# First product of the last feed-forward layer over pairs of token chunks: 512-column matmuls in place of 256-column ones

## The chip, the cores and the metric

The kernel runs on one core of a Trainium2 chip. The metric is the device time of one execution in microseconds (us), lower is better. A core has five engines with instruction queues of their own: TensorE (PE, matrix products; its weight loads are shown as PEld), VectorE (DVE), ScalarE (ACT), GpSimd (POOL) and SyncE (SP, which here issues the transfers). They work side by side and wait for one another through semaphores. Matmuls write to PSUM, eight banks of 128 partitions x 512 fp32 columns.

## The reference

```python
x = A_x                                          # 1 x 2048 x 512
x = x + _A_ref(_layernorm(x), A_wqkv, A_wo)      # linear attention, 32 heads
x = x + _B_ref(_layernorm(x), B_w1, B_w2)        # relu(x @ w1) @ w2, hidden width 1376
x = x + _A_ref(_layernorm(x), A_wqkv, A_wo)
x = x + _B_ref(_layernorm(x), B_w1, B_w2)
```

Linear attention takes `phi(t) = t+1 for t>0, else exp(t)` of queries and keys, multiplies the queries by the sum of key-value products of each head, divides by the normaliser and projects with `wo`. The four layers are numbered 0 to 3; layers 1 and 3 are the feed-forward ones, with the same weights.

## The kernel before

**Tiles and chunks.** The 2048 tokens are 16 tiles of 128, and four chunks of 512 tokens. The residual `xres` stays in SBUF in fp32. Each layer normalises a tile to `xn` (fp16). Pairs of tiles are transposed by DMA from `xn` to `Tb`, so that the feature dimension lies on the partitions: a chunk is complete after two such transposes.

**The end of an attention layer** (function `layer_steps`, steps `bar` and `p2`). The key-value sums are masked to one head each (`kvmask`, L1159) and multiplied into the output weights (`m0` to `m3`), whose four results are evacuated to `Mf`. The projection of tile i (`fin`, four matmuls of 512 columns with weights from `big` and moving data from `Mf`) is added to the residual on VectorE (`resid`, L960). ScalarE squares the row (`sq`, L968). GpSimd and VectorE turn sums into mean, variance, `rstd` and `nbias` for two tiles at once (`ln_stats`); then each tile is normalised (`norm`, L890 on VectorE or GpSimd, L895 on ScalarE), and SP issues the transpose (`tr`, L900). For the four tiles of chunk 0 the projection is split in two halves: the first halves (`fin0_0` to `fin3_0`) and the second ones (`fin0_2` to `fin3_2`), which need `m2` and `m3`. In the tail of `bar` there is also the normaliser of the last chunk (`den3`, four matmuls over 32-column blocks, which the profile shows as `big,Zc`).

**The first product of a feed-forward layer** (`b_h7`). The hidden width of 1376 is split into 2 x 5 feature chunks of 128 (`KH` = 5) and a rest of 96 columns. The rest is computed on its own (`b_h_rest`: `hr`, 16 matmuls of 96 columns a chunk, clipped at zero and transposed by DMA, `trh`). The ten feature chunks are computed by the Winograd form of Strassen's product, with seven block products in place of eight. The blocks of the input are two halves of a chunk's tokens (256 each) by two halves of the 512 features: a11, a12 for the first tokens, a21, a22 for the last. The blocks of the weights are the two halves of the features by the two halves of the hidden width. VectorE makes four sums of the input blocks (`hs1` to `hs4`, L1402, written to `xn`):

    s1 = a21 + a22    s2 = s1 - a11    s3 = a11 - a21    s4 = a12 - s2

Four sums of the weight blocks, t1 to t4, are made once. For each group of feature chunks, `[0,1]`, `[2,3]` and `[4]`, three banks are used. Bank BA takes product 1 (a11), is copied by ScalarE to bank BB (`hv1`, L700), then takes products 6 (s2), 7 (s3) and 4 (a22) on top. BB takes product 2 (a12) on top of the copy. BC takes product 5 (s1), is saved to SBUF (`hv5`, L1455), then takes product 3 (s4). BA is also saved after product 6 (`hv6`). The four results are clipped or added, on ScalarE or VectorE (`hc11`, `hc12`, `hc22`, `hc21`; L1424, L1425, L1436; the clip of two added quarters, `hc22r`, is L1445 or L1446). With two feature chunks a group, a bank holds two blocks of 256 columns, and a product is four matmuls of 256 columns; for the group `[4]` it is two. Products 1 and 2 read the first tokens only; 3 to 7 need the last tokens or the sums.

**The second product** (`b_out`) is a seven-term product too, per chunk, with sums over the hidden values made on VectorE (`b_out_sums`: `ssum1` to `ssum5`, L1509) and terms `p1` to `p7`. `p1` reads the first half of the hidden features for the first tokens, `p5` the sum `ssum1`, `p2` the second half of the features. Its results are added to the residual (L1602), and in the last layer written to staging tiles (L1616, L1610) and stored. `ssum` values are written into the chunk's `Tb` and `xn`.

**The order.** A planner (`_list_schedule`) lays the instructions out for each engine by a priority: the position at which the program text adds the operation, plus a hand-tuned number from the table `HINTS`. `WINDOW` is 1 for every engine, so each engine takes its operations strictly by that sum; entries with `!` choose the engine of an operation that can run on several. Banks are given out as they come free, and semaphore waits follow from reads and writes. The steps of two layers are interleaved: `layer_steps` gives each step the chunk that it needs and the chunk that it provides. Around the start of layer 3 the program text runs: `p2` of chunk 0, first product of chunk 0, `p2` of chunk 1, first product of 1, `p2` of 2, second product of 0, `p2` of 3, first product of 2, second of 1, first of 3, second of 2, second of 3.

Of the kernel before, what the change touches and what calls it, by code (L numbers as in the profile page):

```python
# [7 lines left out]
ALU = alu_op_type.AluOpType  # L8
# [8 lines left out]
C_MM512 = 216.0  # L17
# [45 lines left out]
HINTS = {"0.aqsum1": -43, "0.aqsum1!": 0, "0.aqsum2": -24, "0.aqsum2!": 0, "0.aqsum3": -126, "0.aqsum3!": 0, "0.aqsum4": 36,  # L63
# [545 lines left out]
def build_kernel(nc, A_x, A_wqkv, A_wo, B_w1, B_w2, out, n_layers_pairs=2, K_STT=0, Q_STT=0, windows=None,  # L609
# [20 lines left out]
    with es:  # L630
# [64 lines left out]
        def alloc_bank(cols=512, need=0):  # L695
            return g.new_tile(cols, need)
# [54 lines left out]
        def h_unit(c, t):  # L751
            return c * NCH + t
# [1222 lines left out]
```

## Time and profile before

| | us |
|---|---|
| median of 3 runs (lowest to highest) | 263.33 (263.28 to 263.78) |
| profiled execution, whole time | 262.21 |
| profiled execution, span from first to last instruction | 260.5 |
| TensorE busy / weight loads | 255.3 / 198.9 |
| VectorE busy | 230.7 |
| ScalarE busy | 207.5 |
| GpSimd busy | 60.0 |
| TensorE's granted clock, mean | 1.000 |

Time is counted from the first instruction of the profiled execution. A matmul's own duration in the profile (273 ns for 256 columns, 380 for 512) includes the way through the array, which the next matmul overlaps; what a stream costs is read from the starts of its members. A row such as `177.16 13.11 PE L953 MATMUL ps<-Mf,big 128*128 128x512 bf16 x60` of the engines' order of time gives the start, the length of the stretch, the line, the output tile with its inputs, the shape and how many instructions are merged. All grouped matmuls carry L953, the line of the helper, so their inputs tell them apart: `Tb,w`, `xn,w`, `xn,xin` and `Tb,xin` are the products of layer 3's first product (input blocks or sums by weights or weight sums), `w,Tb` with 96 columns the rest, `w,big` and `xin,big` and the like with bf16 the second product. A SyncE issue is `SPq`; where a DMA's landing matters, the views of a tile give the time from issue to landing.

### The profile page before, as it was taken

The numbers are of one execution on the slowest core, as the hardware profiler recorded it, in microseconds if no ns is written. First come the engines' busy times: TensorE is split into PE (matmuls) and PEld (weight loads), VectorE is DVE, ScalarE is ACT, GpSimd is POOL, SyncE is SP. The second block draws the span as 40 slices with busy tenths as digits, with TensorE's granted clock in tenths as the row PEclk, the third lists the DMA queues.
The fourth block names the chain that finished last, engine by engine and source line by source line (L and its number), as shares of the span: only waits on it lengthen the run. The fifth ranks groups of instructions, "written<-read, shape, count | busy, mean of one in ns | idle before, by whom it ended". The sixth has DMA issues, their size and how long they took to land.

```text
span 260.5 us, 5888 instructions
## 1 busy us (share of the span) xinstructions
PE 255.3 (98%) x2176; PEld 198.9 (76%) x2176; DVE 230.7 (89%) x574; ACT 207.5 (80%) x446; POOL 60.0 (23%) x160
## 2 busy tenths in 40 slices
PE   7999999999999999999999999999999999999995
PEld 3555577834778898889888878774488988988884
DVE  4999998799989999999999899759999997876874
ACT  4999999579989988998899799786999946882200
POOL 4110000028745007240330340002875000000000
PEclk9999999999999999999999999999999999999999
DMA  7767951744351430434031030057442514200104
GB/s 206 277 148 140 330 189 21 183 101 97 68 67 32 87 58 12 91 42 63 0 60 25 0 73 11 3 113 172 95 80 50 82 23 128 56 20 3 81 3 161
DMA packets 45980, 22.46 MB, mean 86 GB/s; under 512 B 35872, under 2 KB 44416, under 8 KB 45952
## 3 DMA queue, kind: packets, MB, share of 16 engines
q1 hardware_dynamic: 45680, 21.83, 35.8%
q8 instruction: 17, 0.28, 0.4%
q10 hardware_dynamic: 272, 0.26, 0.4%
q14 instruction: 11, 0.09, 0.1%
HBM read 7.14 MB, written 2.10 MB: 35 GB/s over the span
## 4 chain that ended last, share of the span: by engine, by line
PE 85%; ACT 5%; DVE 4%; DMA 4%; SPq 1%; issue 1%
PE ps L953 84%; DVE xres L960 2%; DMA Tb<-xn 2%; SPq L1227 1%; ACT sqscr L968 1%; DMA big<-rdc 1%; DMA xin<-in_A_x_dram 1%; ACT xn L895 1%; DVE bst L847 1%; PE ps L914 0%; ACT rdc L1217 0%; DVE big L1235 0%; ACT escr L935 0%; ACT ps L700 0%; ACT lnd L1215 0%
## 5 line engine op out<-in xcount | busy, mean ns | idle before, releaser
L953 PE MATMUL ps<-w,big 128*128 128x256 bf16 (+1 forms) x256 | 32.3, 273 | 0.0
L968 ACT ACTIVATE sqscr<-xres 128x512 bf16<-128x512 f32 x48 | 29.8, 622 | 3.2 <-DVE xres L1623 1.6
L953 PE MATMUL ps<-big,xn 128*128 128x256 bf16 (+1 forms) x224 | 32.1, 288 | 0.0
L700 ACT ACTIVATE ps<-ps 128x512 f32<-128x512 f32 (+1 forms) x41 | 23.1, 573 | 10.5 <-PE ps L953 10.2
L953 PE MATMUL ps<-Mf,big 128*128 128x512 bf16 x128 | 28.6, 380 | 0.0
L953 PEld LDWEIGHTS ps<-w,big 128*128 128x128 bf16 (+1 forms) x256 | 25.0, 98 | 3.1
L953 PEld LDWEIGHTS ps<-big,xn 128*128 128x128 f16 x224 | 21.4, 98 | 6.3 <-issue 1.1
L953 PE MATMUL ps<-Tb,w 128*128 128x256 f16 x160 | 24.3, 273 | 0.0
L1436 DVE TENSOR_TENSOR big<-ps,escr 128x512 bf16<-128x512 f32 (+1 forms) x38 | 22.7, 601 | 1.3 <-ACT escr L1455 0.6
L953 PEld LDWEIGHTS ps<-Mf,big 128*128 128x128 bf16 x128 | 12.2, 98 | 14.5 <-ACT Mf L1166 0.5
L953 PE MATMUL ps<-xn,w 128*128 128x256 f16 x160 | 23.0, 273 | 0.0
L953 PE MATMUL ps<-xn,xin 128*128 128x256 f16 x160 | 22.7, 273 | 0.0
L953 PE MATMUL ps<-wqkv,Tb 128*128 128x512 bf16 (+1 forms) x96 | 20.3, 344 | 0.2 <-ACT Tb L920 0.2
L895 ACT ACTIVATE xn<-xres,nbias,rstd 128x512 f16<-128x512 f32 x24 | 19.1, 813 | 1.4 <-POOL nbias L879 1.4
L1455 ACT ACTIVATE escr<-ps 128x512 f32<-128x512 f32 (+1 forms) x38 | 18.7, 535 | 1.8 <-PE ps L953 1.8
L877 POOL TENSOR_TENSOR rstd<-veps,nhalf 128x2 f32<-128x2 f32 x24 | 18.2, 759 | 7.0 <-DVE veps L875 5.5
L869 POOL TENSOR_SCALAR mean<-s 128x2 f32<-128x2 f32 x24 | 7.2, 301 | 54.4 <-DVE xres L960 52.8
L1424 ACT ACTIVATE big<-ps 128x512 bf16<-128x512 f32 (+1 forms) x38 | 18.9, 527 | 0.4 <-PE ps L953 0.3
L953 PE MATMUL ps<-w,Tb 128*128 128x96 bf16 (+2 forms) x176 | 17.3, 225 | 0.6 <-DMA Tb<-xn 0.6
L953 PEld LDWEIGHTS ps<-Tb,w 128*128 128x128 bf16 x160 | 15.5, 98 | 2.3 <-DVE w L1384 0.2
L1445 ACT ACTIVATE big<-big 128x1024 bf16<-128x1024 bf16 (+1 forms) x16 | 14.3, 904 | 3.5 <-DVE big L1436 3.3
L953 PEld LDWEIGHTS ps<-xn,w 128*128 128x128 bf16 x160 | 15.5, 98 | 1.9 <-DVE xn L1402 0.2
(146 smaller groups left out, 639.6 us busy)
## 6 DMA issues: line engine op xcount, KB each, us to landing
big<-rdc SPq DMA_DIRECT2D x32, 128.0 KB, 2.7
xin<-in_A_x_dram SPq DMA_DIRECT2D x3, 512.0 KB, 7.0
w<-in_B_w_dram SPq DMA_DIRECT2D x1, 1376.0 KB, 7.0
w<-in_B_w_dram SPq DMA_DIRECT2D x1, 1280.0 KB, 10.1
wqkv<-in_A_wqkv_dram SPq DMA_DIRECT2D x3, 256.0 KB, 4.6
wqkv<-in_A_wqkv_dram SPq DMA_DIRECT2D x1, 512.0 KB, 4.5
wo<-in_A_wo_dram SPq DMA_DIRECT2D x1, 512.0 KB, 4.2
out_dram<-GT SPq DMA_DIRECT2D x1, 512.0 KB, 2.6
```

Source lines behind the costliest of these rows:

```text
L700: g.add(ACT, lambda e: e.activation(psv[:, b, 0:w], psv[:, src, 0:w], ACTF.Identity), [("ps", src)], [("ps", b)], C_ACT_PSUM if w == 512 e ...
L847: g.add(DVE, lambda e: e.bn_stats(bst[:, i, :], xin[:, i, :]), [("xin", i)] + list(after), [("bst", i)], C_DVE_BNST, name="bnst%d" % i)
L869: g.add(POOL, lambda e: e.tensor_scalar(mean[:, sl], s1[:, sl], -INV_D, None, ALU.mult), [("s1", i) for i in tl], [("mean", i) for i in tl ...
L877: g.add(POOL, lambda e: e.tensor_tensor(rstd[:, sl], veps[:, sl], nhalf[:, 0:n], ALU.pow), [("veps", lo), ("nhalf",)], [("rstd", i) for i ...
L895: (ACT, lambda e: e.activation(xn[:, i, :], src, ACTF.Identity, scale=rstd[:, i:i + 1], bias=nbias[:, i:i + 1]), C_ACT_SB_AP)],
L953: last = e.matmul(o, l, r, start=st, stop=sp, skip_group_check=skip)
L960: g.add(DVE, lambda e: e.scalar_tensor_tensor(xres[:, i, :], psv[:, b, :], 0.0, src, ALU.add, ALU.add, accum_out=s1[:, i:i + 1]), [("ps", ...
L968: g.add(ACT, lambda e: e.activation(sqscr[:, q, :], xres[:, i, :], ACTF.Square, scale=math.sqrt(INV_D), accum_out=s2[:, i:i + 1]), xr(i), ...
L1424: g.add_flex([(ACT, lambda e: e.activation(ap, src(), ACTF.Relu), C_ACT_PSUM if w == 512 else 270.0), (DVE, lambda e: e.tensor_scalar(ap, ...
L1436: g.add(DVE, lambda e: e.tensor_tensor(ap, sh(psv[:, bank, 0:w]), sh(other()), ALU.add), [("ps", bank)] + okeys + ([] if first else bk), q ...
L1445: g.add_flex([(ACT, lambda e: e.activation(row, row, ACTF.Relu), 945.0 if len(cs) == 2 else C_ACT_SB), (DVE, lambda e: e.tensor_scalar(row ...
L1455: g.add(ACT, lambda e, w=w: e.activation(q[:, 0:w], psv[:, bank, 0:w], ACTF.Identity), [("ps", bank)], key, C_ACT_PSUM if len(cs) == 2 els ...
```

## The change

In layer 3 the first product is computed over pairs of chunks (0 with 1, 2 with 3). The first tokens of the seven-term product are then a whole chunk of 512 tokens, the last tokens the next chunk. Each of the five feature chunks is a group by itself, a bank holds one block of 512 columns, and a product is two matmuls of 512 columns. `b_h7_pair` is `b_h7` with these blocks; the operand sums are 1024 elements a partition. The rest columns of both chunks are added at the head of the pair. Layer 1 keeps the old form (`H_PAIR`).

The steps of layer 3 change with it: the pair (0, 1) needs both chunks and comes after `p2` of chunk 1; the text now runs `p2` of 0, `p2` of 1, first product of 0 and 1, `p2` of 2, second product of 0, `p2` of 3, second of 1, first of 2 and 3, second of 2, second of 3.

The planner gets GpSimd as a third choice for the normalisation of a tile, in all layers. The table of hints is replaced: entries of the old first product go, entries of the new one come, and many of the others have new numbers (181 of layer 0's, 37 of layer 1's, 272 of layer 2's, 100 of layer 3's, and 24 choices of an engine). By position plus hint, TensorE's order at the seam is now:

- before: `den3`, `fin1_0`, `fin2_0`, `m2`, `m3`, `fin0_0`, `fin3_0`, second halves, `fin` of tiles 5, 4, 6, 7, 9, 8, 10, 11, 15, 12, 13, 14, then product 1 of groups [0,1] and [2,3], `hr0`, product 5 of [4], product 2, product 5 twice, product 6 twice of chunk 0
- now: `den3`, `m2`, `m3`, `fin0_0`, `fin1_0`, `fin0_2`, `fin1_2`, `fin3_0`, `fin2_0`, `fin3_2`, `fin2_2`, `fin` of tiles 4 to 8, 11, 9, 13, 12, 10, 14, 15, then product 1 of feature chunks 0 and 1, `hr0`, product 2 of 0 and 1, `hr1`, product 5 of 0 and 1, and so on; at the pair's end product 7 of feature chunk 4, product 4 of 3, `hr2`, `p1` of chunk 0, product 4 of 4, `p5` of chunk 0

VectorE's new order there is: `kvmask1`, a scaling of the queries, `mev2`, another scaling, `resid` 0, 1, a scaling, 3, 2, a scaling, 4, 5, 6, `veps2`, a scaling, 7, `var4`, a scaling, `nbias2`, `veps4`, 8, 9, `var6`, `nbias4`, `veps6`, `norm4`, 11, `nbias6`, 10, 12. ScalarE's is: `sq` 0, 1, 3, 2, 4, `norm1`, `sq5`, `norm0`, `sq7`, `norm2`, `sq6`, `sq9`, `norm5`, `sq8`, `norm6`. `norm3` and `norm7` are on GpSimd, as before.

```diff
-                        (ACT, lambda e: e.activation(xn[:, i, :], src, ACTF.Identity, scale=rstd[:, i:i + 1], bias=nbias[:, i:i + 1]), C_ACT_SB_AP)],
+                        (ACT, lambda e: e.activation(xn[:, i, :], src, ACTF.Identity, scale=rstd[:, i:i + 1], bias=nbias[:, i:i + 1]), C_ACT_SB_AP), ts],
...
+        H_PAIR = {1: False, 3: True}
...
+        def b_h7_pair(q, tw):
+            t1, t2, t3, t4 = tw
+            u0, u1 = 2 * q, 2 * q + 1
+            b_h_rest(u0, 1)
+            b_h_rest(u1, 1)
...
+            lo, hi = slice(4 * u0, 4 * u0 + 4), slice(4 * u1, 4 * u1 + 4)
+            a11, a12, a21, a22 = Tb[:, lo, 0:2, :], Tb[:, lo, 2:4, :], Tb[:, hi, 0:2, :], Tb[:, hi, 2:4, :]
+            kl, kh = [("T", 4 * u0 + i) for i in range(4)], [("T", 4 * u1 + i) for i in range(4)]
...
+                g.add(DVE, lambda e, o=o, a=a, b=b, op=op: e.tensor_tensor(o, a, b, op), rd, wr, C_DVE_TT2, name="%s_p%d" % (nm, q))
+
+            def prod(name, bank, W, X, c, opens, reads):
+                def mk():
+                    return [(psv[:, bank, :], W[:, d, 128 * c:128 * c + 128], X[:, :, d, :], opens and d == 0, d == 1, True) for d in range(2)]
...
+            for c in range(KH):
+                BA, BC = alloc_bank(), alloc_bank()
+                nm = "_p%d_%d" % (q, c)
+                prod("h1", BA, b11, a11, c, True, kl)
+                BB = seed(BA, 512, "hv1" + nm)
+                prod("h5", BC, t1, s1_, c, True, ks[0] + [("uw", 1)])
+                v5 = save("hv5", BC, c)
+                prod("h2", BB, b21, a12, c, False, kl)
+                relu(c, u0, BB, "hc11" + nm)
+                prod("h6", BA, t2, s2_, c, False, ks[1] + [("uw", 2)])
+                v6 = save("hv6", BA, c)
+                prod("h3", BC, b22, s4_, c, False, ks[3])
+                prod("h7", BA, t3, s3_, c, False, ks[2] + [("uw", 3)])
+                add(c + KH, u0, BC, v6, "hc12" + nm)
+                add(c + KH, u1, BA, v5, "hc22" + nm)
...
+                prod("h4", BA, t4, a22, c, False, kh + [("uw", 4)])
+                relu(c, u1, BA, "hc21" + nm)
...
+                if H_PAIR[layer]:
+                    for q in range(NCH // 2):
+                        steps.append((2 * q + 1, None, lambda q=q: h_pair(q)))
+                        for t in (2 * q, 2 * q + 1):
+                            steps.append((NCH - 1 if first_b and t == 0 else None, None if last_layer else t, lambda t=t: o_step(t)))
+                    return steps
```

More of the change, by code (lines that the diff above doesn't have):

```diff
@@ L1835, in h_step, with h_pair @@
                     sums[t] = b_out_sums(t)
+                def h_pair(q):
+                    if not tw7:
+                        tw7.append(w1_sums())
+                    b_h7_pair(q, tw7[0])
+                    for t in (2 * q, 2 * q + 1):
+                        sums[t] = b_out_sums(t)
+                if H_PAIR[layer]:
+                    for q in range(NCH // 2):
+                        steps.append((2 * q + 1, None, lambda q=q: h_pair(q)))
+                        for t in (2 * q, 2 * q + 1):
+                            steps.append((NCH - 1 if first_b and t == 0 else None, None if last_layer else t, lambda t=t: o_step(t)))
+                    return steps
                 for t in range(NCH):
```

29 lines of the change are left out of this document (28 added, 1 removed), and 502 rows, old and new, of the table HINTS.

## The prediction, made before the change was run

> **What bounds the kernel now.** I read the page first, then the chain of waits in order of time, then TensorE's waits, then its order of time around the last feed-forward layer.
>
> ```profile
> PE 255.3 (98%) x2176; PEld 198.9 (76%) x2176; DVE 230.7 (89%) x574; ACT 207.5 (80%) x446; POOL 60.0 (23%) x160
> ...
> 70.18 4.40 DMA Tb<-xn
> 74.58 0.14 issue
> 74.71 183.07 PE ps L953 x1674
> 257.79 0.02 issue
> 257.81 0.43 DVE rdc L1610
> ...
> PE ps L953 <- DMA Tb<-xn: 0.6, 1, 0.6
> ```
>
> The first row is the page's, the next five are the chain of waits (start, length), the last is TensorE's only wait from 74 us on. From 74.71 us to the end 1674 matmuls stand behind one another, 183 us without a gap. So a us of TensorE work saved there is a us of time, and any wait that the change puts in front of a matmul is paid in full. Nothing can be gained there by shortening other engines' work; the hole that ends at 74.71 is the only one left after the start-up and the first attention layer.
>
> TensorE in order of time (start, stretch, count) shows the pace and the place where the last layer begins.
>
> ```profile
> 174.77 0.38 PE L953 MATMUL ps<-wo,KVT 128*128 128x512 bf16 x1
> 175.08 0.40 PE L953 MATMUL ps<-big,Zc 128*32 128x512 bf16 x4
> 175.41 0.62 PE L953 MATMUL ps<-GT,wqkv 128*128 128x128 bf16 x8
> 175.87 1.03 PE L953 MATMUL ps<-Mf,big 128*128 128x512 bf16 x4
> 176.73 0.60 PE L953 MATMUL ps<-wo,KVT 128*128 128x512 bf16 x2
> 177.16 13.11 PE L953 MATMUL ps<-Mf,big 128*128 128x512 bf16 x60
> 190.11 1.04 PE L953 MATMUL ps<-Tb,w 128*128 128x256 f16 x8
> 190.99 0.84 PE L953 MATMUL ps<-w,Tb 128*128 128x96 bf16 x16
> 191.67 0.38 PE L953 MATMUL ps<-xn,xin 128*128 128x256 f16 x2
> ...
> 226.94 2.13 PE L953 MATMUL ps<-xn,xin 128*128 128x256 f16 x18
> 228.90 0.60 PE L953 MATMUL ps<-Tb,w 128*128 128x256 f16 x4
> ```
>
> **Pace: -0.28 us.** The starts of successive rows give the pace. Sixty 512-column matmuls take 190.11 - 177.16 = 12.95 us, 215.8 ns each; eighteen 256-column ones 228.90 - 226.94 = 1.96 us, 108.9 ns. The change takes out 4 chunks x 5 feature chunks x 7 products x 2 = 280 matmuls of 256 columns and puts in 2 x 5 x 7 x 2 = 140 of 512. Each pair becomes 2 x 108.9 - 215.8 = 2.0 ns cheaper: 0.28 us. Rows are rounded to 0.01 us, so 0 to 0.45. That is all that the change can give by itself.
>
> The Trainium skill ("TensorE: Matmul & The Clock Gate", section "Back-to-back issue gap") also gives a sustained figure of about 131 ns for N=512 in a stream with weight loads; by it the 140 matmuls would cost some 12 us less than at 215.8 ns. The 60 matmuls above are such a stream, each with its own weight load, and show 215.8, so I give that result no chance.
>
> **Work off the path: 0.** For each kind of evacuation (VectorE's additions, by form and mean ns, stand for all) the change has ten full 512-column groups instead of eight full and four half ones.
>
> ```profile
> L1436 DVE TENSOR_TENSOR big<-ps,escr 128x512 bf16<-128x512 f32 x12 | 8.1, 685 | 0.3 <-PE ps L953 0.2
> ...
> L1436 DVE TENSOR_TENSOR big<-ps,escr 128x256 bf16<-128x256 f32 x6 | 2.5, 416 | 0.0
> ```
>
> Two full ones for four halves is 1.37 for 1.66 us. The operand sums become eight VectorE additions of 1024 elements (0.69, row at 176.58 below) instead of sixteen of 512 (0.43, row at 196.99 below). So both engines get a little less to do; it is covered by TensorE's full queue either way, with VectorE at 89% and ScalarE at 80%. The hints also move some normalisations to GpSimd (tiles 8 and 12 of the second attention layer, tile 13 of the first feed-forward); their transposes are wanted far later, and GpSimd stands at 23%. Uncovered, each would cost 0.77 to 1.30 us (below).
>
> **The start of the last layer: +0.55 us.** Before, the first product runs on one chunk's transposes. Now, products 3 to 7 of a pair need chunk 1 as well; only products 1 and 2 read chunk 0 alone. The order on TensorE follows from the diff (position in the program plus hint, with no look-ahead): after the last projection matmul of the attention layer come product 1 for two feature chunks, the rest-columns of chunk 0, product 2 twice, then the rest-columns of chunk 1, then product 5. So the work in front of the first need of chunk 1 is 4 x 0.432 + 0.68 (191.67 - 190.99) = 2.41 us, from 190.11 to 192.52.
>
> ```profile
> L900 SPq DMA_TRANSPOSE Tb<-xn x2: 1249/1259/1269, 185.8 to 187.2; - x2
> DMA to landing us min/median/max: 3.1/3.1/3.2
> ...
> L900 SPq DMA_TRANSPOSE Tb<-xn x2: 1232/1260/1289, 192.3 to 193.7; - x2
> DMA to landing us min/median/max: 3.2/3.2/3.3
> ...
> 178.66 0.69 DVE L960 SCALAR_TENSOR_TENSOR xres<-ps,xres 128x512 f32<-128x512 f32 x1
> ...
> 179.28 0.69 DVE L960 SCALAR_TENSOR_TENSOR xres<-ps,xres 128x512 f32<-128x512 f32 x1
> ...
> 184.28 1.50 ACT L895 ACTIVATE xn<-xres,nbias,rstd 128x512 f16<-128x512 f32 x2
> ...
> 187.01 0.61 ACT L968 ACTIVATE sqscr<-xres 128x512 bf16<-128x512 f32 x1
> ...
> 185.67 1.30 POOL L890 TENSOR_SCALAR xn<-xres,mean,rstd 128x512 f16<-128x512 f32 x1
> ...
> 189.86 0.77 POOL L890 TENSOR_SCALAR xn<-xres,mean,rstd 128x512 f16<-128x512 f32 x1
> ...
> 196.99 0.43 DVE L1402 TENSOR_TENSOR xn<-Tb 128x512 f16<-128x512 f16 x1
> ```
>
> Now chunk 1's second transpose is issued at 193.7 and lands at 196.9. Left so, TensorE would wait 4.4 us. The new hints pull it forward. The two matmuls that fold the value mask into the output weights (176.73) come ahead of all projection halves, and tile 0's second half is third among these. The 64 projection matmuls end at 190.11, so they begin 13.81 us earlier at 176.30, tile 0 is complete at 177.6, and its residual addition can start at 177.8 instead of 178.66. VectorE's operations of 0.69 follow each other at 0.62 (178.66, 179.28). In its new order ten stand before the residual of tile 7, which ends at 177.8 + 6.2 + 0.69 = 184.7; that of tile 4 is seventh and ends at 182.2. ScalarE is the slower queue from there: after the square of tile 4 (182.85) come the norm of 1, the square of 5 and the norm of 0 (0.70, 0.62, 0.70), until 184.9; then the squares of tiles 7, 6, 9 and 8 (4 x 0.61), the norms of 2 and 5 (2 x 0.70) and that of 6 (0.80): 189.55. The transpose is issued at 189.65 and lands at 192.85, 0.33 us after TensorE runs dry. Chunk 1's rest-columns (0.68) then run while VectorE makes the first sum of 1024 elements (0.69, and an estimated 0.2 for the hand-overs, as between 175.87 and 176.07), so product 5 waits 0.2 more: 0.55 in all. Ends: 0 if only tile 7's own chain counted (190.5 landed), 1.4 if VectorE does not get its 0.86 us lead. SP's queue holds nothing new ahead of these transposes. What queues behind the wait is all of TensorE's list.
>
> **The step before it: +0.27 us.** Before, the mask of the key-value product is covered by two projection halves (the four matmuls at 175.87). The new order puts only the four normaliser matmuls there.
>
> ```profile
> 176.07 0.42 DVE L1159 TENSOR_TENSOR KVT<-ps,bmask 128x256 bf16<-128x256 f32 x1
> ...
> 176.58 0.69 DVE L1235 TENSOR_TENSOR big<-big 128x1024 bf16<-128x1024 bf16 x1
> ```
>
> The last key-value matmul issues until 175.87, the mask ends at 176.49, the next matmul could start at 176.56: 0.69 us, of which the normaliser matmuls cover 175.41 - 174.99 = 0.42 (mode changes included). 0.27 remain. Ends: 0 to 0.4. The halves still have to run, only behind, so nothing of it comes back.
>
> **The end of the first pair: +0.1 us.** Chunk 0's hidden values are complete only when the pair is, and the second product's fifth term needs the sum over them.
>
> ```profile
> L1509 DVE TENSOR_TENSOR Tb<-big 128x1280 bf16<-128x1280 bf16 x4 | 3.3, 821 | 0.5 <-ACT big L1424 0.5
> ...
> L1359 DVE TENSOR_SCALAR hr<-ps 128x384 bf16<-128x384 f32 x2 | 1.1, 550 | 0.0
> ...
> L1446 DVE TENSOR_SCALAR big<-big 128x1024 bf16<-128x1024 bf16 x2 | 0.8, 416 | 0.0
> ```
>
> VectorE after the last seventh product: 0.2 to see it, 0.62 to add, 0.42 to clip, the rest-columns' clip (ready at 1.31, ends 1.86), the sum 0.82: 2.7 us and 0.1 to hand over. TensorE has, by the new order, two fourth products (2 x 0.43), the rest-columns of chunk 2 (0.68) and the first output product (12 matmuls of 256 columns, 1.31): 2.85. Even, so 0.1, with 0 to 0.4. The second pair ends with more cover (another output product of 10 matmuls, 1.09, for the rest-columns), and the two chunks' sums that VectorE then holds at once fit into the 17 us of output products that remain.
>
> **The sum.** -0.28 + 0 + 0.55 + 0.27 + 0.1 = +0.64 us. The profiled execution is 262.21 us (span 260.5 and 1.7 around it); it becomes 262.85, its span 261.1. The median of the runs, 263.33, is 1.12 above that execution; the same step from there gives 263.97, say 264.0. Its own range, from the terms' ends without the extremes together, is 263.6 to 264.6.
>
> **Rivals.** A difference under 0.2% (0.53 us) can't be told from none.
>
> No new wait: the pulled-forward chain lands in time and the mask is covered. For it: the transposes of chunk 1 need only start 0.5 us earlier than I put them. Against: ScalarE's queue above is full. Then only the pace counts, 263.05.
>
> The hole at 74 us closes as well. It is a transpose that took 4.4 instead of 3.2 us.
>
> ```profile
> q8 instruction: 1, 0.02, 1.3%
> q14 instruction: 1, 0.01, 0.4%
> ...
> Tb<-xn SPq DMA_TRANSPOSE x1, 4.4
> ```
>
> In that window of 5 us an instruction transfer ran beside it. With 3.2 it would have landed 1.2 us earlier and hidden the 0.8 to 0.9 us between the matmuls there. The first attention and feed-forward layers keep their TensorE program and nearly all hints, so the transfer should meet the same transpose; if it doesn't, 263.33 - 0.28 - 0.85 = 262.2. The Trainium skill ("Runtime: NRT & Kernel Launch", "Instruction fetch mechanics") says that an engine's instructions are refilled in blocks of 256 over a DMA queue of its own; TensorE's 2176 matmuls and 2176 loads are exactly 17 such blocks, the page's count on q8, so the block at 72 us should stay where it is.
>
> Chunk 1 arrives late: GpSimd's norm of tile 3 or 7 takes 1.30 instead of 0.77, VectorE's lead is lost, or the transpose itself meets an instruction transfer (1.2). Each alone moves the landing by 0.5 to 1.2 us, all of it paid: 264.0 + 1.2 = 265.2. It decides from the moment the landing passes 192.9.
>
> **How the numbers follow.** My forecast 0.42 (two thirds of it beyond +0.2%), no new wait 0.25, the closed hole 0.14, late chunk 1 0.19. Faster: 0.14 and 0.04 of the second, 0.18. Same: 0.21 of the second and 0.14 of the first, 0.35. Slower: 0.28 and 0.19, 0.47. Range 262.7 to 265.2: it leaves out most of the closed hole and the worst of late landings.
>
> **What would show it.** Right: 240 matmuls of 512 columns become about 380, at 215.8 ns; a wait of 0.3 to 0.6 us in all, on the transposes before chunk 1's rest-columns and on the first sum behind them, some 2.4 us after the last projection matmul; about 0.3 us idle before the output product of the values; the rest of the last layer gapless. Wrong: the transposes land before TensorE runs dry, or TensorE has gaps inside a pair, where I expect none, since each group's chain of evacuations is as long as before.

## The result and the profile after

The changed kernel takes 264.36 us (median of 19 runs, 263.2 to 266.33), the kernel before 262.42 us (19 runs, 261.52 to 263.78) beside it on the same chip. The ratio is 1.0068, with a 95% interval of 1.0053 to 1.0084: 1.8 us slower (1.4 to 2.2). The prediction counted from 263.33 us, the median of three runs of the kernel before; in these 19 runs that kernel has 262.42. The profiled execution of the changed kernel has a span of 262.1 us against 260.5.

The page of the changed kernel, engines' busy times (eleven matmul records are missing, 2025 of 2036):

```profile
PE 254.4 (97%) x2025; PEld 184.4 (70%) x2036; DVE 230.5 (88%) x564; ACT 201.9 (77%) x431; POOL 62.2 (24%) x161
```

TensorE is still what bounds the kernel; the span is longer because TensorE waits more. The chain of waits of the changed kernel (start, length, what):

```profile
70.26 5.31 DMA Tb<-xn
75.57 0.14 issue
75.70 77.66 PE ps L947 x738
...
193.70 0.57 issue
194.28 0.69 DVE xn L1485
194.97 0.05 issue
195.01 64.51 PE ps L947 x476
```

Before, one stretch ran from 74.71 us to 257.78. Now the stretch begins at 75.70, the chain leaves TensorE for a sum on VectorE in front of 195.01, and it ends at 259.52, 1.74 us later. (Where matmul records are missing, from 153 us on, the chain also strays to other engines; those pieces mean nothing.) The first difference comes long before the layer that was changed. TensorE's waits in the changed kernel show it:

```profile
PE ps L947 <- DMA Tb<-xn: 1.5, 1, 1.5
...
PE ps L947 <- DVE KVT L1153: 0.2, 1, 0.2
```

The first row was 0.6 us before. It is the hole at 74 us, in layer 1, where the transpose of chunk 1 now takes 5.31 us in place of 4.40. In TensorE's order of time (the start, the stretch, and in brackets the idle time before it):

```profile
73.82 0.38 PE L947 MATMUL ps<-Tb,w 128*128 128x256 f16 x2
75.70 0.84 PE L947 MATMUL ps<-w,Tb 128*128 128x96 bf16 x16 [1.50 <-DMA Tb<-xn]
```

The DMA view of the changed kernel from 70 to 76 us (queue, packets, MB, share; then the transpose with its us to landing):

```profile
q14 instruction: 2, 0.02, 1.6%
q8 instruction: 1, 0.02, 1.4%
...
Tb<-xn SPq DMA_TRANSPOSE x1, 5.3
```

Before, one packet on q14 ran at 67.5 us, ahead of this transpose, and the next at 73.9. In the changed kernel the two run at 73.5 and 73.9, both inside the transpose.

TensorE in order of time in the changed kernel, at the two places that the prediction named:

```profile
176.56 0.40 PE L947 MATMUL ps<-big,Zc 128*32 128x512 bf16 x4
177.16 0.60 PE L947 MATMUL ps<-wo,KVT 128*128 128x512 bf16 x2 [0.21 <-DVE KVT L1153]
...
191.49 1.03 PE L947 MATMUL ps<-Tb,w 128*128 128x512 f16 x4
192.35 0.84 PE L947 MATMUL ps<-w,Tb 128*128 128x96 bf16 x16
193.03 1.03 PE L947 MATMUL ps<-Tb,w 128*128 128x512 f16 x4
194.05 0.85 PE L947 MATMUL ps<-w,Tb 128*128 128x96 bf16 x16
195.01 1.90 PE L947 MATMUL ps<-xn,xin 128*128 128x512 f16 x8
```

From start to start: the normaliser matmuls take 0.60 us until the next one starts, against 0.33 before (175.08 to 175.41), so the mask costs 0.27. At the entry of the last layer product 2 takes 1.02 against product 1's 0.86 (0.15 of waiting by the single records), and chunk 1's rest-columns 0.96 against chunk 0's 0.68 (0.27): 0.42 in all.

Measured from start to start between TensorE's single matmuls (the "single records" below), the 1.74 us between the two profiled executions divide so:

| where | before | after | difference |
|---|---|---|---|
| start to 74 us | | | +0.12 |
| hole at 74 us | 0.80 | 1.66 | +0.86 |
| mask in the last attention layer | 0 | 0.27 | +0.27 |
| first projection halves behind it (178.3) | 0 | 0.08 | +0.08 |
| last layer, first product to last matmul | 67.66 | 68.02 | +0.36 |

The last row holds +0.42 at the entry, +0.20 in three gaps of 0.05, 0.05 and 0.10 us (197.4, 197.9 and 258.6), and -0.28 of pace. 0.05 us are left over, within the rounding of such sums.

### The profile page after: what moved, and what is told of

Read it like the earlier page. It is cut to its first block, busy times and chain, and to the rows that moved or that the text cites. A ratio compares the mean times of both kernels' runs of the same rounds, so it can differ in the third digit from the quotient of the medians.

```text
span 262.1 us, 5551 instructions
## 1 busy us (share of the span) xinstructions
PE 254.4 (97%) x2025; PEld 184.4 (70%) x2036; DVE 230.5 (88%) x564; ACT 201.9 (77%) x431; POOL 62.2 (24%) x161
## 4 chain that ended last, share of the span: by engine, by line
PE 80%; DMA 6%; ACT 5%; DVE 4%; SPq 2%; issue 1%
PE ps L947 80%; DVE xres L954 2%; DMA big<-rdc 2%; DMA Tb<-xn 2%; DMA xin<-in_A_x_dram 2%; SPq L1221 1%; ACT sqscr L962 1%; ACT lnd L1209 1%; ACT rdc L1211 1%; ACT xn L889 1%; DVE big L1229 1%; DVE bst L841 0%; PE ps L908 0%; ACT ps L694 0%; DVE xn L1485 0%
## 5 line engine op out<-in xcount | busy, mean ns | idle before, releaser
L947 PE MATMUL ps<-big,xn 128*128 128x256 bf16 (+1 forms) x221 | 31.3, 287 | 0.2
L947 PE MATMUL ps<-Tb,w 128*128 128x256 f16 (+1 forms) x120 | 23.6, 308 | 0.0
L947 PE MATMUL ps<-xn,xin 128*128 128x256 f16 (+1 forms) x120 | 22.8, 308 | 0.1
L947 PE MATMUL ps<-xn,w 128*128 128x256 f16 (+1 forms) x120 | 22.1, 308 | 0.0
L947 PEld LDWEIGHTS ps<-xn,w 128*128 128x128 bf16 x120 | 11.3, 98 | 6.1 <-ACT escr L1503 1.7
L947 PEld LDWEIGHTS ps<-xn,xin 128*128 128x128 bf16 x120 | 11.4, 98 | 5.5 <-ACT ps L694 0.6
L947 PE MATMUL ps<-Tb,wqkv 128*128 128x256 f16 (+1 forms) x96 | 15.1, 290 | 0.1
L947 PE MATMUL ps<-xin,Tb 128*128 128x256 bf16 (+1 forms) x96 | 15.2, 272 | 0.0
L927 ACT ACTIVATE big<-ps 128x512 bf16<-128x512 f32 x24 | 15.0, 745 | 0.0
L947 PEld LDWEIGHTS ps<-Tb,w 128*128 128x128 bf16 x120 | 11.6, 98 | 4.9
```

The source lines that it names most:

```text
L927: ops = [g.add(ACT, lambda e: e.activation(dst_ap, psv[:, b, :], ACTF.Identity, bias=1.0 + 1e-6, scale=1.0), [("ps", b)], [dst_key], C_ACT ...
L947: last = e.matmul(o, l, r, start=st, stop=sp, skip_group_check=skip)
```

## The experiments

Line numbers differ by a few between the kernels. Ratios are to the kernel before on the same chip, with 95% intervals.

| kernel | ratio | interval |
|---|---|---|
| the change | 1.0068 | 1.0053 to 1.0084 |
| change, old hints in layers 0 and 1 | 1.0017 | 1.0000 to 1.0034 |
| before, new hints in layers 0 and 1 | 1.0052 | 1.0027 to 1.0076 |
| before, 24 matmuls more at the start | 1.0028 | 1.0007 to 1.0050 |
| before, 15 more | 1.0069 | 1.0047 to 1.0090 |
| change, 24 more | 1.0054 | 1.0032 to 1.0076 |
| change, 15 more | 1.0103 | 1.0068 to 1.0138 |
| change, 512 columns as 2 x 256 | 1.0075 | 1.0043 to 1.0108 |
| change, square of tile 6 earlier | 1.0062 | 1.0040 to 1.0085 |
| change, mask covered by a half | 1.0070 | 1.0044 to 1.0096 |
| change, first sum first | 1.0073 | 1.0048 to 1.0098 |
| change, chunk 0's data for chunk 1 | 1.0096 | 1.0065 to 1.0128 |
| change, old order at the seam | 1.0549 | 1.0515 to 1.0583 |

### Is it the new order in layers 0 and 1?

The change with the 222 old hints of layers 0 and 1 (218 numbers and four choices of an engine), and the kernel before with the 222 new ones. One line after the table of hints does it in each; the second kernel also gets GpSimd as a third choice for a normalisation, which one tile of layer 1 takes.

```diff
+HINTS.update(hints_of_layers_0_and_1)
```

> The changed kernel with the 222 hints of layers 0 and 1 set back to the old ones; layers 2 and 3 stay as changed. Theory: the 0.86 us by which TensorE's hole at 74 us grew comes from the new order in layers 0 and 1 alone, which moves a transpose against the instruction transfers. Then the transpose before the hole takes about 4.4 us again in place of 5.3, TensorE's hole there is 0.8 us in place of 1.66, and the kernel is 0.9 to 1.0 us faster than the changed one, so 0.8 to 0.9 us slower than before (ratio to before about 1.0033). The mask (0.27) and the entry of the last layer (0.42) stay as they are. Rival: the hole grew because the program as a whole has another number of instructions or another layout; then the transpose still takes over 5 us, and the ratio to before stays at about 1.007.

> The kernel before with the new hints in layers 0 and 1 alone (and GpSimd as the third choice for a normalisation, which one tile of layer 1 takes); last layer with 256-column matmuls and layers 2 and 3 in the old order. Theory: the transpose before 74 us takes about 5.3 us, the hole grows from 0.8 to 1.66 us, and the kernel is 0.9 to 1.0 us slower than before (ratio 1.0037) although nothing of the 512-column change is in it. Rival (the program's length or layout moves the transfers): 4.4 us, hole 0.8, ratio 1.000.

The transpose and the hole came out as the theory said, in both. With the old hints the ratio falls to 1.0017 and with the new hints alone it rises to 1.0052; the product is 1.0069, the whole change. That is some 1.4 us each way, where 0.9 to 1.0 was expected. The hole under the change with old hints (TensorE in order of time, then the DMA view from 71 to 76 us):

```profile
74.67 0.38 PE L950 MATMUL ps<-xn,w 128*128 128x256 f16 x2
75.69 0.84 PE L950 MATMUL ps<-w,Tb 128*128 128x96 bf16 x16 [0.64 <-ACT ps L697]
```

```profile
q14 instruction: 1, 0.01, 0.4%
...
Tb<-xn SPq DMA_TRANSPOSE x1, 4.5
```

75.69 - 74.67 less two matmuls (0.22) is 0.80 us, the hole of before. In the kernel before with the new hints the chain of waits has the long transpose, and the DMA view from 71 to 77 us again two packets on q14:

```profile
71.32 5.22 DMA Tb<-xn
```

```profile
q14 instruction: 2, 0.02, 1.6%
```

Its hole is 1.84 us by the single records, although its last layer has the old product and takes 67.66 us as before. So some three quarters of the loss (0.52 of 0.68%) come from orders in two layers whose work was not changed. The ratio left with the old hints, 1.0017, has an interval that reaches 1.0000, so the runs alone hardly tell it from none.

The spans of the two profiled executions show less than the runs do. With the old hints it is 262.0 us, no shorter than the change's 262.1, because TensorE comes to the hole 0.97 us later than in the profile of before; that execution, of 263.80 us, is one of the slower of its kernel (median 263.16). With the new hints alone TensorE comes to the hole 0.92 us later, 0.54 of it in a wait at 63 us. What differs ahead of the hole is not explained here.

The hole isn't the same in each execution. With the old hints the three profiled executions that keep the start as it was or add 15 matmuls have 0.80 each; with the new ones it was 1.66, 1.72, 1.74, 1.84 and twice 2.0, but also 1.18 (mask covered by a half) and 0.79 (chunk 0's data), where the transfer on q8 or the second one on q14 came at another moment. The one profile of the change shows a common case, and the ratios of many runs carry the verdict.

### Is it the instruction transfer that lengthens the transpose?

```diff
-                for k in range(WARM):
-                    last = e.matmul(psv[:, wt, :], wrm[:, 0:128], wrm[:, :], start=True, stop=True)
+                for k in range(4 * WARM):
+                    last = e.matmul(psv[:, wt, 0:128], wrm[:, 0:128], wrm[:, 0:128], start=True, stop=True)
```

> The kernel before; only the eight 512-column warm-up matmuls at its start are issued as 32 of 128 columns, the same columns in all. That puts 24 more matmuls in front of TensorE's program, so the instruction transfer that ran at 72.0 us is fetched some 24 matmuls of 109 ns (2.6 us) earlier, at 69.4, and is over when the transpose before the hole is issued at 70.2. Theory (the instruction transfer lengthens the transpose): it takes 3.2 to 3.3 us in place of 4.4, lands at 73.5, the hole of 0.80 us closes, and the kernel is 0.7 to 0.9 us faster than before (ratio 0.997). Rival (the transpose is lengthened by other transposes, or by something else at this place): still 4.4 us, a hole of 0.8, ratio 1.000.

> The same split of the warm-up matmuls in the changed kernel. The transfer on q8 moves from 71.2 to about 68.6 us; the two on q14 (73.5 and 73.9) stay. Theory that q8's transfer costs most: the transpose lands at 73.5 to 73.8, the hole of 1.66 us falls to 0 to 0.4, and the kernel is 1.2 to 1.6 us faster than the changed one, so within 0.5 us of before. Theory that q14's pair, which before has only one of, costs as much: the transpose still takes 4.2 to 4.5 us, the hole is 0.6 to 0.9, and the gain 0.7 to 1.0 us. Rival (neither): nothing moves.

The hole closed, but nothing was won. The kernel before with 24 more, TensorE in order of time where the hole was, the DMA view from 70.5 to 74 us, and the chain of waits:

```profile
74.02 0.38 PE L953 MATMUL ps<-xn,w 128*128 128x256 f16 x2
74.24 0.84 PE L953 MATMUL ps<-w,Tb 128*128 128x96 bf16 x16
```

```profile
q14 instruction: 1, 0.01, 0.9%
...
Tb<-xn SPq DMA_TRANSPOSE x1, 3.0
```

```profile
103.47 4.84 DMA Tb<-xn
...
194.09 5.23 DMA Tb<-xn
199.34 0.43 DVE xn L1402
```

The transfer moved to 68.0 us, the transpose at 70.73 took 3.0 us, and TensorE went on without a wait. But the transfers that now ran at 106.0 and 197.5 us met the transposes issued at 103.47 and 194.09: 4.84 and 5.23 us where before 3.31 and 3.30 were needed. TensorE paid 0.87 and 1.38 us there, more than the 0.80 that it got back. So the mechanism is shown in both directions: where the transfer leaves a transpose, it gets shorter, and where one comes in, longer. The expected gain was not to be had, because I had not asked what the other transfers would meet.

In the changed kernel the transpose fell from 5.31 to 3.94 us with q8's transfer gone and q14's two left, and the hole from 1.66 to 0.28: between the two theories, so q14's pair alone came with some 0.9 us of lengthening (3.94 - 3.03). What q8 does alone so early in a transpose (0.97 us after the issue in the change) is seen in three others. It started 1.26 and 1.34 us after the issues at 90.95 and 91.60 in the two kernels with 24 more, which took 4.24 and 4.33 us, and 1.11 us after the issue at 211.12 in the kernel with the old seam, which took 4.08. So q8's earlier moment alone does not give 5.31. In the change and the six other kernels in which this transpose took 4.8 to 5.5 us, it landed 1.6 to 1.7 us after the start of the second packet on q14. The longer transpose thus goes with that packet, though no experiment moved it alone.

And in the changed kernel too a wait opened where none was, behind the transpose issued at 104.12 (4.94 us): 0.97 us by the single records, in two pieces. In TensorE's waits the larger one appears under VectorE, which waited for the data first:

```profile
PE ps L947 <- DVE big L1016: 0.6, 1, 0.6
```

Transposes of two tiles, issue to landing in us, and the start of each instruction transfer near them, from the traces' single records:

| kernel | issued | took | q8 at | q14 at |
|---|---|---|---|---|
| before | 70.18 | 4.40 | 72.0 | 73.9 |
| the change | 70.26 | 5.31 | 71.2 | 73.5, 73.9 |
| change, old hints in 0 and 1 | 71.03 | 4.53 | 72.7 | 74.9 |
| before, new hints in 0 and 1 | 71.32 | 5.22 | 72.3 | 74.6, 75.0 |
| before, 24 more | 70.73 | 3.03 | | 73.4 |
| change, 24 more | 70.82 | 3.94 | | 72.9, 73.8 |
| before, 24 more | 194.09 | 5.23 | 197.5 | |
| before, 15 more | 12.65 | 4.99 | 15.6 | |

With a smaller shift I tried to miss all of them:

```diff
-                for k in range(WARM):
+                for k in range(3):
                     last = e.matmul(psv[:, wt, :], wrm[:, 0:128], wrm[:, :], start=True, stop=True)
+                for k in range(20):
+                    last = e.matmul(psv[:, wt, 0:128], wrm[:, 0:128], wrm[:, 0:128], start=True, stop=True)
```

> The kernel before with 15 more matmuls at its start in place of 24 (three warm-up matmuls of 512 columns and 20 of 128, the same columns in all). With 24, the transfers on q8 moved from 72.0 to 68.0, from 110.0 to 106.0 and from 200.4 to 197.5 us, so with 15 they should run at 69.5, 107.5 and 198.6: after the transposes that end at 70.4, 107.3 and 197.0 or in front of the packets of the one issued at 70.2. Theory: no transpose that TensorE or VectorE waits for is lengthened, the 0.8 us hole at 74 us closes, none opens at 109 and 199 us, and the kernel is 0.7 to 0.9 us faster than before (ratio 0.997). Rival: moving the transfers always meets some transpose, and the sum stays at the time of before or above (ratio 1.000 to 1.003).

> The changed kernel with the same 15 matmuls more. The transfers on q8 that ran at 71.2 and 111.1 us should run at 69.2 and 108.4, clear of the transposes before 74 and 109 us; the two on q14 at 73.5 and 73.9 stay. Theory: the hole of 1.66 us falls to 0.3 to 0.5, nothing opens at 109 us, and against the kernel before with the same 15 matmuls what is left is the change itself: 0.27 (mask) + 0.42 (entry) + 0.19 (small gaps) - 0.28 (pace) + 0.3 to 0.5 (rest of the hole) = 0.9 to 1.1 us slower; so about 1.0005 of the time of before. Rival: a wait opens elsewhere and the ratio is over 1.004, as with 24.

Both rivals held: nothing was won, and the kernel before with 15 more has 1.0069, above even the 1.003 that its rival allowed. The chain of waits of the kernel before with 15 more:

```profile
12.65 4.99 DMA Tb<-xn
...
72.54 4.40 DMA Tb<-xn
```

The first transfer came at 15.6 in place of 17.8 us, met the first transpose of the kernel (3.26 us before) and cost 1.9 us at once. The one at the hole did not move against its transpose at all (74.3 with the issue at 72.54, as 72.0 with 70.18), so the hole stayed. In the changed kernel the same early transpose took 5.09 us; the hole fell to 0.26, and the wait at the entry of the last layer was about 0.55. When a transfer comes is thus not a mere count of matmuls, and I can't place it. No version that beats the kernel before was found.

### What is the width itself worth?

```diff
-return [(psv[:, bank, :], W[:, d, 128 * c:128 * c + 128], X[:, :, d, :], opens and d == 0, d == 1, True) for d in range(2)]
+return [(psv[:, bank, 256 * p:256 * p + 256], W[:, d, 128 * c:128 * c + 128], X[:, 2 * p:2 * p + 2, d, :], opens and p == 0 and d == 0, d == 1, True) for p in range(2) for d in range(2)]
```

> The changed kernel with each of the pair's 140 matmuls of 512 columns issued as two of 256 columns on the two halves of the same bank, in the same place; all else is as changed. Theory: the width by itself is worth 2.0 ns a pair of matmuls, so 140 x 2.0 = 0.28 us; the kernel is 0.2 to 0.5 us slower than the changed one, with TensorE gapless between 198 and 256 us as there. Rival: wider matmuls save more, because a weight load less is issued for each (140 loads fewer); if a load that is not hidden cost 20 ns, the kernel would be 2.8 us slower. Second rival: no difference at all, within 0.1 us.

From the pair's first matmul to the last of the kernel the split version takes 68.34 us against 68.02: 0.32 us, where 0.28 were expected. The ratio (1.0075) can't tell this from the change's 1.0068; its hole at 74 us is 1.74. No cost of the 140 more weight loads shows.

### The mask

```diff
-    '2.fin2_0': 12,
+    '2.fin2_0': -8,
```

> The changed kernel with one projection half (the first of tile 2) moved ahead of the two matmuls that fold the value mask into the output weights. Theory for the mask: the 0.27 us of idle time there closes, because 0.43 us of work now lies over it. Theory for the entry: tile 0 is then complete 0.43 - 0.27 = 0.16 us later, and the chain residual, square, statistics, normalisation to chunk 1's second transpose starts from there, so the wait at the entry grows by up to 0.43 (TensorE is dry 0.27 earlier, the transpose 0.16 later): the kernel between 0.27 us faster and 0.16 us slower than the changed one, and the sum of the two waits is what the new order trades, not either alone. Rival: the mask is no term at all; the idle time stays, because the half itself waits for an evacuation.

TensorE in order of time in this kernel:

```profile
175.98 0.40 PE L950 MATMUL ps<-big,Zc 128*32 128x512 bf16 x4
176.63 0.60 PE L950 MATMUL ps<-Mf,big 128*128 128x512 bf16 x2 [0.24 <-ACT Mf L1163]
...
192.45 1.08 PE L950 MATMUL ps<-Tb,w 128*128 128x512 f16 x4
193.93 0.85 PE L950 MATMUL ps<-w,Tb 128*128 128x96 bf16 x16 [0.40 <-DMA Tb<-xn]
```

The rival held: 0.65 us between the first two rows as against 0.60, and what ends it is now ScalarE's evacuation of the second masked product, which the half needs. Two operations end about together there, and covering one bares the other; before, the four small matmuls over `GT` stood between. The entry's wait grew to some 0.6 us, as the chain argument said, since tile 0 was complete later. The price of 0.27 is right, but it isn't the mask's alone.

### The entry of the last layer

```diff
-    '2.sq6': 4, '2.norm6': 15,
+    '2.sq6': -3, '2.norm6': 7,
```

> The changed kernel with two hints of ScalarE moved: the square of tile 6 goes ahead of the normalisation of tile 2, and the normalisation of tile 6 ahead of the square of tile 8. Theory: chunk 1's second transpose is held by ScalarE's queue, so it is issued 0.5 to 0.7 us earlier (190.3 in place of 190.92) and lands at 193.4; the waits at the entry (0.15 on the transpose and 0.27 on the first sum, 0.42 in all) go, and the kernel is 0.4 us faster than the changed one. Rival: VectorE's or GpSimd's chain for tile 7 holds the transpose, and nothing changes. Second rival: chunk 0's second transpose, whose tile 2 is now later by one square (0.6 us), lands after TensorE is dry at 191.5, the wait moves to chunk 0's rest-columns, and the kernel is 0 to 0.3 us slower.

Chunk 1's second transpose was issued 0.56 us before the first product, as in the changed kernel (0.57), and the last layer took 68.05 us. Two rows of this kernel's order of time, ScalarE and GpSimd, show why:

```profile
190.56 0.81 ACT L892 ACTIVATE xn<-xres,nbias,rstd 128x512 f16<-128x512 f32 x1 [0.34 <-DVE nbias L876]
```

```profile
190.52 0.76 POOL L887 TENSOR_SCALAR xn<-xres,mean,rstd 128x512 f16<-128x512 f32 x1
```

The normalisation of tile 6 now waits for VectorE's `nbias`, which stands in its queue behind residual additions, and GpSimd's normalisation of tile 7 ends at the same time anyway. The rival held: not ScalarE alone, as I had it, but three engines bind within 0.3 us of each other.

Then the transpose against the sum: once with chunk 1's data replaced by chunk 0's, once with the sum ahead of the clip.

```diff
-            b_h_rest(u1, 1)
+            b_h_rest(u1, 1, 0 if q == 0 else u1)
...
+            if q == 0:
+                hi = lo
...
```

> The changed kernel with the first pair's rest-columns of chunk 1 and its operands a21 and a22 read from chunk 0's tiles, so nothing in the first pair of layer 3 waits for chunk 1's transposes (chunk 1's own hidden values are left out). Theory A, as predicted: the transposes cause the entry's whole wait; without them the rest-columns start 0.15 us earlier and the first sum is ready in time, so 0.42 us faster than the changed kernel. Theory B: the first sum stands on VectorE behind the clip of product 2, which ends at 194.28 us because it waits for TensorE, so the sum can't come earlier; the 0.15 us in front of the rest-columns only moves in front of product 5, and the kernel is 0 to 0.05 us faster.

```diff
-    '3.hs1_p0': 39,
+    '3.hs1_p0': 34,
```

> The changed kernel with the first operand sum of the pair ahead of the clip of product 2 in VectorE's order, on true data. Theory B (the clip holds the sum): the sum runs from 194.05 in place of 194.28, product 5 waits 0.05 in place of 0.27 us, 0.2 us faster, if the clip, now 1 us later, holds no bank that a matmul wants. Theory A (the transpose alone holds it): nothing changes at the entry. Rival: the late clip opens a wait of its own some 2 us on, and nothing is won.

With chunk 0's data, TensorE and VectorE in order of time:

```profile
192.95 0.84 PE L947 MATMUL ps<-w,Tb 128*128 128x96 bf16 x16
194.07 1.90 PE L947 MATMUL ps<-xn,xin 128*128 128x512 f16 x8 [0.27 <-DVE xn L1488]
```

```profile
192.72 0.69 DVE L1500 TENSOR_SCALAR big<-ps 128x512 bf16<-128x512 f32 x1 [0.34 <-PE ps L947]
193.33 0.68 DVE L1488 TENSOR_TENSOR xn<-Tb 128x1024 f16<-128x1024 f16 x1
```

Theory B: the wait before the rest-columns is gone, the one behind them is 0.44 us (1.12 - 0.68), and the sum is as large as with the transpose (0.42). VectorE waits for TensorE's product 2, clips it, and only then makes the sum. (This kernel also has a wait of 1.08 us at 209.4 for a sum of the second product. Its cause is not known; it outweighs the smaller hole, 0.79 in place of 1.66.) With the sum first, on true data, TensorE and VectorE:

```profile
194.73 1.04 PE L950 MATMUL ps<-xn,xin 128*128 128x512 f16 x4
195.93 1.04 PE L950 MATMUL ps<-xn,xin 128*128 128x512 f16 x4 [0.16 <-DVE xn L1488]
```

```profile
193.98 0.69 DVE L1488 TENSOR_TENSOR xn<-Tb 128x1024 f16<-128x1024 f16 x1 [0.71 <-DMA Tb<-xn]
194.59 0.68 DVE L1500 TENSOR_SCALAR big<-ps 128x512 bf16<-128x512 f32 x1
195.19 0.68 DVE L1488 TENSOR_TENSOR xn<-xn,Tb 128x1024 f16<-128x1024 f16 x1
```

Theory B again, and its rival too: the wait behind the rest-columns falls from 0.27 to 0.04 us, but the clip now stands between the first and the second sum, product 6 waits 0.33 us for the latter, and the last layer takes 68.19 us in place of 68.02. The 0.42 us are held by the transpose and by VectorE's order at once.

### The old order at the seam

```diff
+HINTS.update(hints_of_layer_2_before)
```

> The changed kernel with layer 2's hints as before (288 entries), so the attention layer's end runs in the old order under the paired first product. Theory: the mask is covered again (0.27 us less), but chunk 1's second transpose is issued some 3 us later than in the changed kernel, and TensorE waits 3.5 to 4.5 us in front of chunk 1's rest-columns: 3.2 to 4.2 us slower than the changed kernel, 5 to 6 us slower than before. Rival: the pair would have been entered as early without the new order, and the new hints of layer 2 only cost the mask; then 0 to 0.3 us faster than the changed kernel.

TensorE's waits and its order of time at the entry:

```profile
PE ps L950 <- DMA Tb<-xn: 10.1, 3, 5.2
```

```profile
199.89 0.85 PE L950 MATMUL ps<-w,Tb 128*128 128x96 bf16 x16 [3.12 <-DMA Tb<-xn]
200.62 3.03 PE L950 MATMUL ps<-xn,xin 128*128 128x512 f16 x8
```

In front of chunk 1's rest-columns 3.28 us are lost, with 0.6 us more in the products ahead of them: 3.9, as expected, and the mask's 0.27 is covered. So the pair needs the new order of layer 2: without it the entry alone costs 3.9 us. The whole kernel became 14 us slower, far more than expected: at the second pair another 5.3 us are lost on a transpose (the longest of the three waits is 5.2), and after both waits TensorE ran at a lower clock (below).

## Why the prediction was right, and where not

**The time.** 264.0 us was forecast and 264.36 measured, inside the range, but so near by luck. The forecast was a step of +0.64 on 263.33; the step is +1.8 on 262.42. The base was 0.9 too high and the step 1.2 too small, and the two errors nearly cancel. That the kernel gets slower, by waits at the seam, was right; what made most of the loss was not among the terms.

**Bound and pace.** TensorE's list was the bound, and waits were paid in full: right. The pace, -0.28, was right (the split version shows 0.32).

**The step before the last layer.** +0.27 predicted, 0.27 measured. The cause is wider than I said: the evacuation of a masked product ends at the same time as the mask.

**The start of the last layer.** +0.55 predicted, 0.42 measured. The transpose was expected 0.33 us after TensorE ran dry, and came 0.15 after; the first sum 0.2 later, measured 0.27. ScalarE's queue is not the only limit, as the square moved forward showed, and the sum has a second one, the clip that waits for product 2. The added waits have the size that I gave them, but neither went away by the one move tried on each.

**The end of the first pair.** +0.1 predicted, nothing there: TensorE has no wait at the pair's end. The three small gaps in the last layer, 0.20 us, are elsewhere; two of them lie inside the first pair, where I had expected none.

**What failed: the hole at 74 us.** I gave layers 0 and 1 no term, on the sentence that they "keep their TensorE program and nearly all hints, so the transfer should meet the same transpose". "Nearly all hints" was wrong: 218 of them have new numbers, as the list of the change says. The transfer did meet the same transpose, but 1.0 us after its issue in place of 1.8, and a second packet on q14 came with it; the transpose took 0.9 us longer, and the hole grew by 0.86. I had counted only with this hole closing. The exchange of hints in both directions shows that these hints carry 0.52% (0.27 to 0.76), some 1.4 us. In the profiled executions the hole is 0.86 to 1.04 of it. Where the rest lies is not shown: ahead of the hole the executions differ by up to 1 us, with the old hints too.

**The sum.** The terms that I had, with 0.42 for 0.55 and 0 for 0.1, give -0.28 + 0.42 + 0.27 = +0.41; with the small gaps (0.20 + 0.08) +0.7. The change with the old hints in layers 0 and 1 measures +0.45 us (0 to 0.9), so my +0.64 is within its interval. Of the missing 1.1 us, 0.86 are the hole in the profiled pair. The section that the prediction cites there (the Trainium skill, "Runtime: NRT & Kernel Launch", section "Instruction fetch mechanics") also says that the cost of crossing a block is mostly hidden. For TensorE itself the trace agrees: before, 13 such transfers on q8 run between 74.71 us and the end without a wait of TensorE. For a transpose in flight the cost is not hidden: 3.0 us without the transfer, 4.4 and 5.3 with it.

## What to carry to other kernels

A change to one layer that comes with a new order for the others has to be costed there too; run the old order under the new code and the new order under the old code before the difference is put down to the code. Where the bound engine has one long stretch, any transfer that lands just in time is a risk of a us or two, and it depends on what else the DMA queues carry in those few us, instruction transfers included. Where several engines end within 0.3 us of each other, moving one operation forward shows another limit instead of a gain.

## What the runs showed of the hardware

**Instruction transfers lengthen transposes.** In the thirteen kernels other than the one with the old seam, from 55 us on, 210 transposes of two tiles had no instruction packet under way between issue and landing: 3.0 to 3.4 us each. Fourteen had a 16 KB packet on q8 that started 0.9 to 2.4 us after the issue: 4.2 to 5.5 us, all of them, while the packet itself took 0.9 to 1.5. (The kernel with the old seam has two more, 5.4 and 4.1.) A packet of 8 KB on q14 alone, started 1.8 to 2.3 us after the issue, left 3.6 to 3.8 in 11 cases. One on q8 that started between 0.9 us before the issue and 0.4 us after it left 3.0 to 3.3, or up to 3.85 where a q14 packet came too; from 2.5 to 3.4 us after it some took 4.7 to 5.2 and others 3.0 to 3.3, and what sets them apart I can't say. Nor does the profile say whose instructions q14 carries, or why the new hints brought two of its packets together.

**A wait of 3 us costs again afterwards.** The kernel with the old order at the seam, TensorE's clock by stretch (window, length, PE, PEld, DVE, ACT and POOL busy, clock, DMA share, GB/s):

```profile
196.00:200.00 4.00, 0.71 (x5) 0.22 (x6) 0.79 (x2) 1.34 (x4) 1.97 (x6) 1.00 0.69 131
200.00:205.00 5.00, 5.00 (x29) 2.24 (x29) 3.02 (x5) 3.24 (x8) 0.00 (x0) 0.66 0.13 26
205.00:215.00 10.00, 10.00 (x47) 4.08 (x46) 9.57 (x22) 7.58 (x16) 3.38 (x6) 1.00 0.37 42
...
222.00:225.00 3.00, 3.00 (x17) 2.03 (x15) 2.65 (x5) 0.13 (x1) 0.00 (x0) 0.50 0.00 0
```

After the wait of 3.1 us the granted clock was 0.66 as a mean of five us, with 512-column matmuls starting 427 ns apart for a while (216 otherwise), and after the longer one 0.50 over three. The trace's own clock records have 0.50 from 201.24 to 204.65 us and from 218.30 to 225.13: the first drop came 1.35 us after TensorE had started again. The waits of 0.2 to 2.0 us, in this kernel and the others, left it at 1.00. The Trainium skill ("TensorE: Matmul & The Clock Gate", section "HAM oscillation — how this bites in real kernels") gives no gaps over about 3.4 us as the rule; the trace agrees in kind, though here a wait of 3.1 us by the profile's count, 3.3 from start to start less the matmul, was enough.
